# Diagonal score blocks as 64 by 64 squares, and the order of all steps written out as a list

## The chip, the cores and the metric

The kernel runs on one core of one Trainium2 chip. The metric is the device time of one execution in microseconds, the median over several runs.

## The reference

Two layers, each an attention A with a memory of earlier segments and then a feed-forward block B, on 2048 tokens of width 640:

```python
x = x + A(layernorm(x));  x = x + B(layernorm(x))      # and the same once more
# A: 32 heads of width 20, 4 segments of L = 512 tokens, M and z carried from segment to segment
logits = einsum('bhqd,bhkd->bhqk', qs, ks) * 20**-0.5 + mask    # causal within the segment
a_dot  = einsum('bhqk,bhkd->bhqd', softmax(logits), vs)
a_mem  = (phi(qs) @ M) / (phi(qs) @ z + 1e-6)          # phi(t) = t + 1 if t > 0 else exp(t)
o      = sigmoid(beta) * a_mem + (1 - sigmoid(beta)) * a_dot;   M += phi(ks).T @ vs;  z += sum phi(ks)
# B: relu(x @ w1) @ w2, hidden width 1728
```

## The kernel before

All activations are bf16 in SBUF; `x_sb` holds the tokens in 16 tiles of 128 partitions. Every step is a Python generator ("stream") that yields operations: scores, exponentials, causal masking, value sums, projections, memory reads and writes, the feed-forward block, loads and stores. A planner (`Sched`) holds a modelled clock per engine, picks at each step the stream whose operation can start first, moved by a hand-tuned table of shifts (`SHIFT`), and appends the operation to its engine's queue. What comes out is one fixed instruction order for TensorE (PE), VectorE (DVE), ScalarE (ACT), GpSimd (POOL) and SyncE (SP), with semaphores between them.

Matmuls come in three tile shapes of the 128 by 128 array. "Full" uses all of it. "cols" uses four column tiles of 32 (projections cut into quarters at L777, value sums at L1397): four matmuls side by side. "rows" uses four row tiles of 32 (scores at L1301): a head has 20 features, so four heads run side by side, each into its own PSUM bank. Projections and the feed-forward block exist as full (L774) and as four column tiles (L777), and the planner takes the shape that the array is in.

Scores are computed transposed: keys on partitions, queries on columns. A pair of groups (z = 0, 1; four heads each) takes five rounds; a round fills two slots of two PSUM banks with 512 columns per head:

```python
ROUNDS = (((0, 0, 0),), ((0, 1, 0), (0, 3, 384)), ((0, 2, 0), (1, 2, 256)),
          ((1, 0, 0),), ((1, 1, 0), (1, 3, 384)))        # (z, key block j, column in the bank)
```

Key block j of 128 keys is taken against the queries from 128*j on, so that a segment has 512 + 384 + 256 + 128 = 1280 columns per head. Per round ACT applies two exponentials (L1365, 128 partitions by 1024 elements) from PSUM into `PT`. POOL then zeroes the upper part of each diagonal 128 by 128 block (affine select, L1377), and the value sums (L1397) multiply `PT` by the values, four matmuls per key block, 16 per group. There are 32 pairs, 160 rounds. The two slots of a round have to be read by ACT before the next round can be written; a third slot is lent to the scores in the first segment only.

The scores read `pad`, to which SP copies q and k from a DRAM scratch `scr` (L1117), to which it copied the projections before (L1070). SP also issues the transposes, the weight loads (w1 at L643), the loads of x (L609, L618, L635) and the stores (L1642, L1646), all in the order of its own queue.

Of the kernel before, what the change touches and what calls it, by code (L numbers as in the profile page):

```python
# [7 lines left out]
ALU = mybir.AluOpType  # L8
# [27 lines left out]
PT_OFF = [0, 512, 1024, 896]  # L36
# [73 lines left out]
class Op:  # L110

    def __init__(self, alts, waits, dma=None, acq=None, urgent=False, take=(), mode="full", lag=0.0, port=False):
        self.lag = lag
# [8 lines left out]
        self.urgent = urgent  # L125
        self.take = take
        self.data = 0.0
# [32 lines left out]
class Spawn:  # L160
    def __init__(self, prio, gen):
        self.prio = prio
        self.gen = gen


LONE_NS = 300.0
SWITCH_NS = 96.0
COLS_LAG = 1500.0
SOFT = 400
SOFT_DMA = 1000  # L170
SOFT_FROM = ("sc",6,4,1)
SEM_NS = 60.0
PE_MARGIN = 80.0
HOLDERS = 1
SHIFT = {
# [41 lines left out]
}  # L217
HOLD_TOL = {"pe": 220.0, "act": 150.0, "dve": 200.0, "pool": 0.0, "sp": 0.0}


class Sched:


    def __init__(self, prog):
        self.P = prog
        self.free = {e: 800.0 for e in ENGS}
        self.t = {}
        self.events = {}
        self.streams = []
        self.dma_free = 0.0  # L230
        self.rank = {}
        self.mode = "full"
        self.soon = 0.0
        self.landed = set()
        self.met = {}
        self.seen = {}
        self.phase = {}
        self.made = {}
        self.held = {"dve": [], "pool": []}

    def add(self, prio, gen):
        self.streams.append([prio, gen, None, None, False])
        self.rank[id(gen)] = 0
# [8 lines left out]
    def enter(self, gen, phase):  # L252
        if self.phase.get(id(gen)) != phase:
            self.phase[id(gen)] = phase
            self.made[id(gen)] = 0

    def place(self, n, gen):
        k = self.made.get(id(gen), 0)
        return n, self.phase.get(id(gen), 0), sum(k >= x for x in (6, 20, 60))

# [6 lines left out]
    def _fill(self, st):  # L267
        while st[2] is None and not st[4]:
            try:
                y = next(st[1]) if st[3] is None else st[1].send(st[3][0])  # L270
            except StopIteration:
                st[4] = True
                return
            st[3] = None
            st[2] = y

    def _settle(self, st):

        while True:
            self._fill(st)  # L280
            if st[4]:
                return False
            y = st[2]
            if isinstance(y, (Op, Either)):
                return True
            if isinstance(y, Spawn):
                self.add(y.prio, y.gen)
                self.rank[id(y.gen)] = self.rank[id(st[1])]
                st[2], st[3] = None, (None,)
            elif isinstance(y, Need):  # L290
                if y.key not in self.events:
                    return False
                st[2], st[3] = None, (self.events[y.key],)
            else:
                s = self._pick(y.slots)
                if s is None:
                    return False
                s.free = False
                st[2], st[3] = None, (s,)
# [5 lines left out]
    def _mode(self, op):  # L305
        if op.cols is None:
            return op.mode
# [1437 lines left out]
```

## Time and profile before

| | |
|---|---|
| time, median of 3 runs | 551.09 us (550.83 to 551.12) |
| span of the profiled execution | 549.3 us |
| PE busy | 539.8 us, 98% |
| ACT busy | 406.0 us, 74% |
| DVE busy | 427.8 us, 78% |
| POOL busy | 195.7 us, 36% |
| score matmuls (L1301) | 1024 |
| exponentials (L1365) | 320, 1028 ns each |

The profiled execution has no time of its own besides its span, from the first to the last instruction; the runs' times also contain what lies around it. Busy PE time is the union of matmul records, which are pipelined: a record holds the columns and a tail, so that two neighbours overlap, and a busy PE may do less than it could. What a matmul occupies is read from the distance between starts. PE is idle mostly in the first 20 us.

### The profile page before, as it was taken

How to read it: one execution, taken by the hardware profiler on the slowest of the kernel's cores; microseconds unless marked ns; L12 is line 12 of the kernel's file. 1: busy time of each engine (PE TensorE's matmuls, PEld its weight loads, DVE VectorE, ACT ScalarE, POOL GpSimd, SP SyncE). 2: the span in 40 equal slices, each digit the busy share in tenths (PEclk: the TensorE clock that was granted, in tenths of full speed). 3: DMA queues.
4: the chain of work that ended last, by engine and by line, in shares of the span. 5: the costliest groups of instructions: out<-in, count | busy, mean ns of one | idle time of the engine just before them, and what ended most of it. 6: DMA issues, size and time to landing. Idle time of an engine off the chain costs nothing.

```text
span 549.3 us, 20483 instructions
## 1 busy us (share of the span) xinstructions
PE 539.8 (98%) x9025; PEld 305.5 (56%) x9025; DVE 427.8 (78%) x1067; ACT 406.0 (74%) x516; POOL 195.7 (36%) x305
## 2 busy tenths in 40 slices
PE   7999999999999999999999999999999999999997
PEld 6543464455554546646556555564646654757656
DVE  4899999898999989898778858997899788417102
ACT  5699899789888987788888867897778787350130
POOL 5255444333453334443433423433333333201000
PEclk9999999999999999999999999999999999999999
DMA  8699979715384175438384743336246511541201
GB/s 270 165 198 253 245 158 223 221 44 116 89 165 98 40 180 77 75 68 120 47 212 93 116 116 93 58 69 104 50 139 130 117 32 22 106 63 33 71 2 51
DMA packets 133325, 62.20 MB, mean 113 GB/s; under 512 B 112116, under 2 KB 123124, under 8 KB 133236
## 3 DMA queue, kind: packets, MB, share of 16 engines
q1 hardware_dynamic: 132672, 60.36, 51.5%
q8 instruction: 71, 1.16, 0.9%
q10 hardware_dynamic: 564, 0.53, 0.4%
q14 instruction: 18, 0.15, 0.1%
HBM read 20.56 MB, written 12.85 MB: 61 GB/s over the span
## 4 chain that ended last, share of the span: by engine, by line
PE 88%; ACT 6%; DVE 2%; DMA 2%; SPq 1%; issue 0%
PE ps L774 35%; PE ps L777 35%; PE ps L1301 8%; PE ps L1397 6%; ACT PT L1365 5%; PE ps L1180 2%; DMA x_sb<-in_A_x_dram 1%; PE ps L1572 1%; PE ps L1238 1%; DMA pad<-scr 1%; SPq L602 1%; DVE xn_tok L841 0%; SPq L612 0%; DVE stats L795 0%; DVE x_sb L1614 0%; DVE o_sb L1491 0%
## 5 line engine op out<-in xcount | busy, mean ns | idle before, releaser
L1365 ACT ACTIVATE PT<-ps 128x1024 bf16<-128x1024 f32 x320 | 308.9, 1028 | 59.3 <-PE ps L1301 57.6
L1377 POOL TENSOR_SCALAR_AFFINE_SELECT PT<-PT 128x512 bf16<-128x512 bf16 x256 | 169.3, 679 | 241.1 <-ACT PT L1365 241.0
L777 PE MATMUL ps<-xnT,w_r 128*32 128x512 bf16 x1256 | 76.0, 379 | 0.0
L777 PE MATMUL ps<-w_r,hT 128*32 128x320 bf16 (+1 forms) x1764 | 67.8, 295 | 0.0
L1614 DVE TENSOR_TENSOR x_sb<-x_sb,ps 128x320 bf16<-128x320 bf16 (+1 forms) x65 | 30.7, 474 | 43.6 <-PE ps L777 38.7
L1301 PE MATMUL ps<-pad 20*128 20x512 bf16 (+3 forms) x1024 | 63.4, 301 | 1.2 <-ACT PT L1365 0.7
L774 PE MATMUL ps<-w_r,hT 128*128 128x320 bf16 x404 | 64.2, 300 | 0.0
L795 DVE BATCH_NORM_STATS2 stats<-x_sb 128x6 f32<-128x320 bf16 x124 | 55.0, 478 | 3.8 <-DMA x_sb<-in_A_x_dram 3.0
L777 PEld LDWEIGHTS ps<-w_r,hT 128*32 128x32 bf16 x1764 | 45.2, 97 | 12.6 <-issue 1.4
L1595 ACT ACTIVATE hT<-ps 128x512 bf16<-128x512 f32 x50 | 29.9, 599 | 29.0 <-PE ps L777 25.6
L774 PE MATMUL ps<-xnT,w_r 128*128 128x512 bf16 x206 | 50.8, 380 | 0.0
L774 PEld LDWEIGHTS ps<-w_r,hT 128*128 128x128 bf16 x404 | 37.6, 98 | 19.4 <-issue 4.9
L1301 PEld LDWEIGHTS ps<-pad 20*128 20x128 bf16 x1024 | 17.9, 92 | 52.9 <-issue 24.5
L777 PEld LDWEIGHTS ps<-xnT,w_r 128*32 128x32 bf16 x1256 | 31.6, 97 | 27.8 <-issue 2.0
L1519 DVE TENSOR_TENSOR x_sb<-x_sb,ps 128x320 bf16<-128x320 bf16 x64 | 29.7, 478 | 20.4 <-PE ps L777 16.0
L811 POOL TENSOR_TENSOR rstd<-lnU,mhalf 128x2 f32<-128x2 f32 (+2 forms) x27 | 21.1, 782 | 63.5 <-DVE lnU L807 60.4
L1407 DVE CAST otu<-ps 128x512 bf16<-128x512 f32 x52 | 35.6, 685 | 9.1 <-PE ps L1397 8.2
L1397 PE MATMUL ps<-PT,v_aug 128*21 128x128 bf16 (+3 forms) x896 | 40.3, 300 | 0.0
L1594 DVE TENSOR_SCALAR hT<-ps 128x512 bf16<-128x512 f32 x54 | 36.5, 681 | 1.7 <-PE ps L774 0.7
L1491 DVE TENSOR_TENSOR o_sb<-otk,rden 128x320 bf16<-128x320 bf16 x62 | 34.8, 588 | 0.5
L981 DVE CAST stg<-ps 128x512 bf16<-128x512 f32 (+1 forms) x37 | 24.7, 669 | 12.5 <-PE ps L774 6.3
L1146 ACT ACTIVATE stg<-stg 128x512 bf16<-128x512 bf16 x50 | 31.7, 635 | 2.0 <-DVE rtmp L1144 1.8
(118 smaller groups left out, 731.5 us busy)
## 6 DMA issues: line engine op xcount, KB each, us to landing
pad<-scr SPq DMA_DIRECT2D x124, 80.0 KB
scr<-stg SPq DMA_DIRECT2D x34, 256.0 KB, 2.5
out_dram<-x_sb SPq DMA_DIRECT2D x15, 160.0 KB, 1.9
w_r<-in_B_w_dram SPq DMA_DIRECT2D x10, 216.0 KB, 4.0
w_r<-in_B_w_dram SPq DMA_DIRECT2D x13, 160.0 KB, 2.8
x_sb<-in_A_x_dram SPq DMA_DIRECT2D x10, 160.0 KB, 3.2
scr<-w_r SPq DMA_DIRECT2D x5, 256.0 KB, 4.2
wv_r<-in_A_wv_dram SPq DMA_DIRECT2D x1, 800.0 KB, 9.7
```

Of the source, the lines that this page charges most:

```text
L774: return e.matmul(view(dst.ap, b), a, b, start=(k == 0), stop=(k == last))
L777: return e.matmul(view(dst.ap[rows], b), part, b, start=(k == 0), stop=(k == last))
L795: tk = yield dve(320, 1, lambda e, c2=c2: e.bn_stats(stats6[:, t, c2, :], x_sb[:, t, c2 * 320:(c2 + 1) * 320]), xt)
L1146: te = yield act(512, lambda e, q=q: e.activation(q, q, ACT.Exp), [tr] + p, psum=False)
L1301: fns.append([(lambda e, z=z, j=j, hh=hh, N=N, o=o, sl=sl, q=hh % 2: e.matmul(slot.ap[:, q, o:o + N], sl.ap[32 * hh:32 * hh + DH, z, 0, 12 ...
L1365: tx = yield act(1024, lambda e, dst=dst, src=src: e.activation(dst, src, ACT.Exp, scale=SCALE), sc + pw)
L1377: tm = yield pool(600.0, lambda e, reg=reg: e.affine_select(out=reg, in_=reg, pattern=[[0, 4], [1, 128]], compare_op=ALU.is_ge, fill=0.0, ...
L1397: fns.append((lambda e, OD, j=j, hh=hh: e.matmul(OD.ap[32 * hh:32 * hh + DH + 1, 128 * j:L], VAUG[vx(a, s)][:, j, 4 * g + hh, :], pt.ap[:, ...
L1407: te = yield evac(L, 1, lambda e: e.tensor_copy(dst, OD.ap), lambda e: e.activation(dst, OD.ap, ACT.Copy), [tk] + OTU[0].tks)
L1491: to = yield dve(320, 1, lambda e, z=z, dst=dst: e.tensor_tensor(dst, av[:, z, :, :, 0:DH], rd.ap[:, z].to_broadcast([128, NJ, 4, DH]), AL ...
L1594: th = yield evac(512, 1, lambda e: e.tensor_scalar(hT[:, dc, :], bk.ap[:, :], 0.0, None, ALU.max), lambda e: e.activation(hT[:, dc, :], b ...
L1614: ta = yield dve(n, 1, lambda e: e.tensor_tensor(x_sb[:, t, c0:c0 + n], x_sb[:, t, c0:c0 + n], bk.ap[:, 0:n], ALU.add), [tk], urgent=True)
```

## The change

**Squares.** The diagonal block of 128 by 128 is cut into four squares of 64 by 64, and the one in which all keys are later than all queries is not computed any more. The rounds of a pair now are: two for z = 0, one shared round with the eight pairs of diagonal squares of both groups, two for z = 1. A square is a matmul of 64 keys by 64 queries in a 32 by 64 tile ("halves": four row tiles by two column tiles), 32 of them in the shared round. So that the squares of an even and an odd key block lie on different halves of the partitions, the odd token tiles are kept with their two halves swapped, from the load of x to the store of the result; each affected load or store is split by partition halves.

**Buffers.** `PT` keeps 1280 columns per head, in another order, and the squares that are not computed are cleared to zero once (two POOL memsets). The shared round's exponentials are four of 512 elements on 64 partitions, in place of two of 1024 on 128. POOL makes eight selects per pair as before, on blocks of 64 columns. The value sums take five segments of 512, 128, 256, 256 and 128 columns, 20 matmuls for 16.

**Order.** The planner's choice, its table of shifts and its priorities are gone. A string `ORDER` lists the number of the stream that goes next at each step, and whether it takes its second form (another engine, or column tiles). The model of the clock stays, for the choice among free buffers.

The built programs have 9025 and 11807 matmuls: the scores' go from 1024 to 2304, the value sums' from 992 to 1240, and 400 full matmuls of the projections and the feed-forward block become four column tiles each (1359 full at L774 before, 959 after).

```diff
-PT_OFF = [0, 512, 1024, 896]
+PT_AT = {(0, 0): 0, (0, 1): 128, (0, 2): 256, (0, 3): 384, (3, 3): 512, (2, 2): 640, (2, 3): 768,
+         (1, 2): 896, (1, 3): 1024, (1, 1): 1152}
+SUMS = ((0, 0, 512, 0), (3, 512, 128, 384), (2, 640, 256, 256), (1, 896, 256, 256), (1, 1152, 128, 128))
+FULLS = (((0, 64, 448), (3, 384, 64)), ((2, 320, 192), (1, 256, 256), (1, 128, 64)))
+FULL_AT = (64, 704)
+DIAG = ((0, 0, 0), (0, 3, 448), (1, 2, 256), (1, 1, 192))
...
+ORDER = """
+37*2 36*3 37 35 37 36 37*2 36 35 37 21*3 35 21 26 21*3 26 22*2 21 22 26*3 37*3 22 28*2 21 37 28*2 21 28 23*2 148 28*5
...
+        blocks = PT[:].rearrange("p z h (y c) -> p z (h y) c", y=2)
...
+        def pair_loads(t):
+            return [lambda e, p=p: e.dma_start(x_sb[p:p + 64, t:t + 2, :], bass.AP(
+                tensor=A_x.tensor, offset=A_x.offset + (128 * t + p) * D,
+                ap=[[D, 64], [(192 if p == 0 else 64) * D, 2], [1, D]])) for p in (0, 64)]
...
+            t2 = yield pool(1200, lambda e: e.memset(blocks[:, :, :, 0:64], 0.0))
+            t3 = yield pool(1200, lambda e: e.memset(blocks[:, :, :, 576:640], 0.0))
...
-        ROUNDS = (((0, 0, 0),), ((0, 1, 0), (0, 3, 384)), ((0, 2, 0), (1, 2, 256)),
-                  ((1, 0, 0),), ((1, 1, 0), (1, 3, 384)))
+        ROUNDS = ((0, 0), (0, 1), (None, None), (1, 0), (1, 1))
...
+                if zn is None:
+                    parts = [(z, 64 * (j % 2), q0, 64, q0, 64, 256 * y + 64 * z) for z in range(2) for y, j, q0 in DIAG]
+                else:
+                    parts = []
+                    for j, q0, nq in FULLS[w]:
+                        parts.append((zn, 0, 128 * j, 128, q0, nq, o))
+                        o += nq
...
-                    return pe(233.0, fns, a[1] + b[1] + a[0].tks + b[0].tks, take=[a[0], b[0]], mode="rows"), None
+                    on = ROUNDS[HALVES[h][1]][0] is None
+                    return pe(135.0 if on else 233.0, fns, a[1] + b[1] + a[0].tks + b[0].tks, take=[a[0], b[0]],
+                              mode="halves" if on else "rows")
...
+                        if z is None:
+                            src = bkp.ap.rearrange("p h (y x) -> p (h y) x", y=2)[:, :, 0:128].rearrange(
+                                "p e (z c) -> p z e c", z=2)
+                            moves = [(blocks[rows, :, 4 * k:4 * k + 4, c0:c0 + 64], src[rows])
+                                     for rows, c0 in ((slice(0, 64), 0), (slice(64, 128), 576))]
...
+            def clear(z, rows, c0, base, ex):
+                reg = blocks[rows, z, :, c0:c0 + 64]
+                return pool(600.0, lambda e: e.affine_select(
+                    out=reg, in_=reg, pattern=[[0, 2 * 4], [1, 64]], compare_op=ALU.is_ge, fill=0.0, base=base,
+                    channel_multiplier=-1), ex)
...
-            for j in range(NJ):
+            for y, (j, c0, nq, q0) in enumerate(SUMS):
                 for hh in range(4):
...
-            OD, tk = yield pe(540.0, fns, mk + vt, acq=MISC, mode="cols", lag=COLS_LAG)
+            OD, tk = yield pe(545.0, fns, mk + vt, acq=MISC, mode="cols")
```

More of the change, by code (lines that the diff above doesn't have):

```diff
@@ L110, with __init__ @@
 class Op:
-    def __init__(self, alts, waits, dma=None, acq=None, urgent=False, take=(), mode="full", lag=0.0, port=False):
-        self.lag = lag
+    def __init__(self, alts, waits, dma=None, acq=None, take=(), mode="full", port=False):
         self.port = port
@@ L454, in pe, with _times @@
-def pe(ns, fns, waits=(), acq=None, take=(), mode="full", lag=0.0):
-    return Op([("pe", ns, fns, 190.0)], waits, acq=acq, take=take, mode=mode, lag=lag)
+    def _times(self, op, k, waits):
+        e, hold, fns, tail = op.alts[k]
+        m = PE_MARGIN if e == "pe" else 0.0
+        if e == "pe" and op.mode == "cols" and op.cols_ns is not None:
+            hold = op.cols_ns
+        if e == "pe" and op.mode != self.mode:
+            hold = hold + SWITCH_NS
+        start = max([self.at(t) + SEM_NS + m for t in waits], default=0.0)
+        start = max(self.free[e], start)
+        if e == "dve" and op.port:
+            for a, b in self.held["pool"][-6:]:
+                if a <= start + 66.0 < b:
+                    hold = max(hold, b - start + op.data - 70.0)
+        if e == "pool":
+            for a, b in self.held["dve"][-6:]:
+                if a < start + hold and b > start:
+                    hold = hold + b - max(a, start)
+        return start, start + hold
@@ new lines, in run @@
+    def run(self):
+        tops = list(self.streams)
+        first = tops[0]
+        self._settle_all()
+        for word in ORDER.split():
+            code, _, count = word.partition("*")
+            for _ in range(int(count or 1)):
+                n, other = int(code) % 80, int(code) >= 80
+                st = tops[n] if n < 40 else next(x for x in self.kids[id(tops[n - 40])] if not x[3])
+                self._record(st, st[1].fn() if isinstance(st[1], Either) else st[1], other)
+                self._settle(st)
+                self._settle_all()
+                if isinstance(first[1], Either):
+                    first[1].fn()
+        assert not self.streams
@@ new lines, in _record @@
+    def _record(self, st, op, other):
+        k = int(other and len(op.alts) > 1)
+        e, _, fns, tail = op.alts[k]
+        if op.cols is not None:
+            op.mode = "cols" if other else "full"
+            fns = op.cols if other else fns
+        waits, slot = op.waits, None
+        for s in op.take:
+            s.free = False
+        if op.acq is not None:
+            slot = self._pick(op.acq)
+            slot.free = False
+            waits = waits + slot.tks
+            fns = [(lambda eng, fn=fn, slot=slot: fn(eng, slot), mark) for fn, mark in fns]
+        start, end = self._times(op, k, waits)
+        self.P.waits(e, waits)
+        self.free[e] = end
+        if e == "pe":
+            self.mode = op.mode
+        if e == "dve" and op.port:
+            self.held[e].append((end - op.data, end))
+        elif e == "pool":
+            self.held[e].append((start, end))
+        if op.dma is not None:
+            tk = self.P.dma(e, fns[0][0], op.dma)
+            self.dma_free = max(self.dma_free, start + 300.0) + tail[1]
+            self.t[(id(tk[0]), tk[1])] = max(self.dma_free, end) + tail[0]
+            if tail[2]:
+                self.free[e] = max(end, self.dma_free)
+            out = tk
+        else:
+            marks = []
+            for fn, mark in fns:
+                tk = self.P.op(e, fn, mark)
+                if tk is not None:
+                    self.t[(id(tk[0]), tk[1])] = end + tail
+                    marks.append(tk)
+            out = marks[0] if len(marks) == 1 else (marks or None)
+        st[1], st[2] = None, ((slot, out) if slot is not None else out,)
@@ L458, in either, with pe @@
+def pe(ns, fns, waits=(), acq=None, take=(), mode="full"):
+    return Op([("pe", ns, fns, 190.0)], waits, acq=acq, take=take, mode=mode)
 def either(op, cols, ns=None):
@@ L617, in loads @@
                     yield Need("warmed")
-                yield from ld(("sp", "act")[t // 2], "x0%d%d" % divmod(t, 2), 163840, lambda e, t=t: e.dma_start(
-                    x_sb[:, t, :], xs[:, t, :]))
+                tks = []
+                for fn in one_load(t):
+                    tk = yield dma(("sp", "act")[t // 2], sem_("d_x0%d%d" % (t, len(tks))), 81920 if t % 2 else 163840,
+                                   fn, lat=1470.0)
+                    tks.append(tk)
+                S.set("x0%d%d" % divmod(t, 2), tks=tks)
             tz = yield Need("beta0")
@@ L633, in x_pieces @@
             def x_pieces(s):
-                def one(t):
-                    return lambda e: e.dma_start(x_sb[:, t, :], xs[:, t, :])
-                return [("x%d%d" % (s, i), 163840, one(4 * s + i)) for i in range(4)]
+                return [("x%d%d" % (s, i), 163840, fn) for i in range(2) for fn in pair_loads(4 * s + 2 * i)]
             def rows(name, w, src, k):
@@ L933, in proj_ln @@
             if a == 0:
-                xw = [[("x10",)]] * 2 + [[("x11",)]] * 2 if s == 1 else [[("x%d%d" % (s, i),)] for i in range(NJ)]
+                xw = [[("x10",)]] * 2 + [[("x11",)]] * 2 if s == 1 else [[("x%d%d" % (s, i // 2),)] for i in range(NJ)]
             else:
@@ L1286, in half @@
                 m, u, k = HALVES[h]
-                parts = ROUNDS[u]
+                zn, w = ROUNDS[u]
                 pd = []
-                for z in {z for z, _, _ in parts}:
+                for z in range(2) if zn is None else (zn,):
                     n = 2 * m + z
@@ L1352, in exps @@
                         pts.append(pt)
-                    pw = [t for z, _, _ in parts for t in pts[z].tks]
+                    pw = [t for pt in (pts if z is None else pts[z:z + 1]) for t in pt.tks]
                     ex = []
@@ L1609, in ffn @@
             hrest = yield Need("hR", b, s)
-            sums = [[] for _ in range(NJ)]
             def residual(i, hf, bk, tk, c0, n):
@@ new lines, in store @@
+            if s < NSEG - 1:
+                return
+            t = TT - 2
+            tks = yield Need("xB", b, s, NJ - 2)
+            S.last = yield dma("sp", dout, 163840, lambda e, t=t: e.dma_start(
+                out[0, t * 128:(t + 1) * 128, :], x_sb[:, t, :]), tks)
+            t, i = TT - 1, NJ - 1
+            for hf, u, c0, n in ((0, 0, 0, 320), (1, 0, 320, 160), (2, 0, 480, 160)):
+                tks = yield Need("sum", b, s, 2 * i + hf)
+                for k, (p, r) in enumerate(halves(t)):
+                    S.last = yield dma(("sp", "act")[k], dout, 128 * n, lambda e, p=p, r=r, c0=c0, n=n: e.dma_start(
+                        out[0, t * 128 + r:t * 128 + r + 64, c0:c0 + n], x_sb[p:p + 64, t, c0:c0 + n]), tks)
@@ new lines, in items @@
+        def items(f, count):
+            for n in range(count):
+                yield from f(n)
+        S.add(scores())
+        S.add(exps())
+        S.add(items(causal, NSEG * G))
+        S.add(items(apply, 2 * NSEG * G))
+        S.add(each(free_v))
+        S.add(items(turn_pair, NSEG * G))
+        S.add(items(divide, NSEG * G))
+        S.add(each(turn_o))
+        S.add(each(out_proj(0)))
+        S.add(each(out_proj(1)))
+        S.add(each(ln_b(0)))
+        S.add(each(ln_b(1)))
+        S.add(each(fill))
@@ L1712, in bass_interleave_layers__memory_aug_infini_attn__dense_activation_relu__prompt_kernel @@
+        S.add(each(proj_v))
+        S.add(each(ffn))
+        S.add(each(ffn_rest))
+        S.add(each(store))
+        S.add(warm_pe())
+        S.add(consts())
+        S.add(loads())
+        S.add(late_loads())
         S.run()
```

594 lines of the change are left out of this document (262 added, 332 removed), and 41 rows, old and new, of the table SHIFT.

## The prediction, made before the changed kernel ran

> **What bounds the kernel now.** I read the page's parts 1, 2 and 4 first, then the windows view, then the timeline of TensorE alone.
>
> ```profile
> span 549.3 us, 20483 instructions
> PE 539.8 (98%) x9025; PEld 305.5 (56%) x9025; DVE 427.8 (78%) x1067; ACT 406.0 (74%) x516; POOL 195.7 (36%) x305
> PEclk9999999999999999999999999999999999999999
> PE 88%; ACT 6%; DVE 2%; DMA 2%; SPq 1%; issue 0%
> ```
>
> TensorE (PE) is busy 98% at the full clock, and the chain that ended last is 88% PE. The three runs have a median of 551.09 us, 1.8 above this span; I make the sum against the span and carry the 1.8 over.
>
> ```profile
> 0.00:20.00 20.00, 16.37 (x162) 12.50 (x162) 12.06 (x36) 9.89 (x27) 8.06 (x26) 1.00 0.73 223
> 20.00:31.00 11.00, 11.00 (x126) 5.77 (x122) 10.48 (x31) 10.36 (x15) 4.97 (x7) 1.00 0.95 204
> 31.00:65.00 34.00, 32.19 (x462) 14.31 (x457) 31.70 (x79) 32.10 (x37) 19.16 (x29) 1.00 1.02 240
> 65.00:75.00 10.00, 9.76 (x81) 5.46 (x82) 9.80 (x25) 8.85 (x12) 3.35 (x5) 1.00 0.98 189
> 75.00:150.00 75.00, 75.00 (x1098) 40.19 (x1096) 68.53 (x170) 65.47 (x82) 30.84 (x47) 1.00 0.60 139
> 150.00:470.00 320.00, 319.19 (x5111) 175.08 (x5114) 273.24 (x678) 260.47 (x316) 126.63 (x188) 1.00 0.49 98
> 470.00:546.00 76.00, 76.00 (x1996) 52.13 (x2000) 21.65 (x54) 18.82 (x31) 2.69 (x5) 1.00 0.23 49
> ```
>
> The first number after each stretch's length is PE's busy time. Outside the first 20 us PE is idle 1.81 us in 31 to 65, 0.24 in 65 to 75, 0.81 in 150 to 470, and nowhere else. So the kernel is PE's own work plus three microseconds. Only 31 to 65 has another limit: ScalarE (ACT) is busy 32.10 of 34 there, and the chain of waits is ACT for nearly all of it:
>
> ```profile
> 33.96 25.71 ACT PT L1365 x28
> 59.67 0.10 SPq L643
> ...
> 59.81 0.43 SPq L1070
> 60.28 0.43 SPq L1070
> ...
> 60.76 4.43 DMA pad<-scr
> ...
> 65.24 0.39 PE ps L1301 x4
> ```
>
> 28 exponentials back to back, then a `pad` transfer that is issued only behind a piece of w1 and two `scr` stores on SP, and lands at 65.19. A busy PE may still waste array time, so its cost per step is read from starts:
>
> ```profile
> 300.66 0.59 PE L774 MATMUL ps<-xnT,w_r 128*128 128x512 bf16 x2
> 301.19 0.39 PE L1301 MATMUL ps<-pad 20*128 20x512 bf16 x4
> 301.51 0.73 PE L1572 MATMUL ps<-xnT,w_r 128*32 128x256 bf16 x20
> 304.34 2.33 PE L774 MATMUL ps<-xnT,w_r 128*128 128x512 bf16 x10
> ...
> L774 PE MATMUL ps<-xnT,w_r 128*128 128x512 bf16 x206 | 50.8, 380 | 0.0
> ```
>
> Ten 512-column matmuls take 2.33 us, the last one 0.38 (the mean in the last row: 0.21 of columns and a tail of 0.17): 0.217 between starts, which is 2.4 columns per ns (213 ns) and 3 ns. Two of them from 300.66 are done feeding at 301.09; the score matmuls start at 301.19, and four of them side by side (32-row tiles) let the next tile shape start 0.32 later, not 0.22. **A change of tile shape costs about 0.10 us each way**: 0.10 in, 0.107 out.
>
> **The change, part by part.** Counts are from the order of the two built programs; 32 pairs of head groups, five score rounds each, four heads side by side.
>
> *Squares.* Round 2 had 512 columns in two waves of four matmuls (256 and 256); now 32 matmuls of 64 columns, eight side by side if the 32 by 64 tiles run together: four waves, 256 columns, 107 ns of array time less. But a wave costs more than its columns:
>
> ```profile
> 181.30 0.29 PE L1301 MATMUL ps<-pad 20*128 20x256 bf16 x4
> 181.42 0.28 PE L1301 MATMUL ps<-pad 20*128 20x256 bf16 x4
> 147.31 0.33 PE L1238 MATMUL ps<-v_aug,phk 128*32 128x42 bf16 x24
> ```
>
> A wave of 256 columns in row tiles (107 ns) is followed 0.12 later by the next: 13 ns over. In column tiles (third row: six waves of four, 42 and 63 columns, each matmul with its own weights) 24 matmuls take 0.33; less the last one's 0.19 (a tail of 0.17 and its columns) that is 0.14 for five steps, 28 ns each where the columns need 26. So weights reload at that pace, and the excess lies between 2 and 13 ns a wave. The squares have both kinds of tile, and a round that is over at a wave's last matmul; I take the row tiles' 13, the nearest, for each of three inner steps and 13 more for the eight matmuls' stagger. New round: 107 + 39 + 13 = 159 ns; old: 213 + 13 = 226. Gain 67 ns, times 32: **-2.15 us**. At 3 ns a step without stagger it is 116 ns (-3.5); if the two 64-column halves do not run together, eight steps of 27 + 13 make 320 ns (+3.0).
>
> *The other rounds* keep 512 columns in more waves: 448 and 64 for one of 512, 192, 256 and 64 for 384 and 128. One step of 13 ns more in each of 4 x 32 rounds: **+1.66** (bounds 0.26 at 2 ns, 3.4 at twice 13).
>
> *Shape changes*: 322 before, 330 now, the eight more between full and column tiles: 8 x 0.10, **+0.8** (bounds 0 and 0.9).
>
> *Value sums* (L1397): five segments of the same 1280 columns for four, 62 times, 3 ns: **+0.2**. Full matmuls turned into four column tiles keep their columns: nothing.
>
> *ScalarE.* The square round's two exponentials of 1024 become four of 512 on 64 partitions.
>
> ```profile
> L1365 ACT ACTIVATE PT<-ps 128x1024 bf16<-128x1024 f32 x320 | 308.9, 1028 | 59.3 <-PE ps L1301 57.6
> 329.05 1.94 ACT L1365 ACTIVATE PT<-ps 128x1024 bf16<-128x1024 f32 x2 [0.81 <-PE ps L1301]
> L982 ACT ACTIVATE stg<-ps 128x512 bf16<-128x512 f32 x30 | 18.0, 600 | 5.4 <-PE ps L777 3.1 <-PE ps L774 1.8
> 331.39 0.40 PE L1301 MATMUL ps<-pad 20*128 20x512 bf16 x4
> 331.72 1.53 PE L774 MATMUL ps<-wv_r,xnT 128*128 128x320 bf16 x10
> 331.82 1.94 ACT L1365 ACTIVATE PT<-ps 128x1024 bf16<-128x1024 f32 x2 [0.51 <-PE ps L1301]
> 334.22 0.40 PE L1301 MATMUL ps<-pad 20*128 20x384 bf16 x8
> ```
>
> Two take 1.94, so the next starts after 0.91 and 0.12 of each is hidden; 512 at 600 ns then steps by 0.48. Four: 1.92, two: 1.82, **0.1 us more per pair, 3.3 us of ACT in all, hidden**: the score matmuls end earlier by 0.07, and the rows show the cover: the exponentials of 331.82 end at 333.76 and the next round starts at 334.22, 0.46 later. With that cover gone PE would pay up to 3.3. Where ACT does set the pace (31 to 65, 14 rounds, three of them squares) it is 0.3, and the new order has two ACT copies fewer ahead of round 16, at 0.48 each: nil.
>
> *GpSimd.* Eight selects of 512 elements per pair as before (two on 64 partitions), and two clearings of 1024 elements once. For group 0 two selects now follow the square round's exponentials, where one did: 0.68 later for its value sum.
>
> ```profile
> L1377 POOL TENSOR_SCALAR_AFFINE_SELECT PT<-PT 128x512 bf16<-128x512 bf16 x256 | 169.3, 679 | 241.1 <-ACT PT L1365 241.0
> 9.51 0.73 POOL L701 MEMSET maskg<- 128x756 bf16 x1 [0.68 <-DVE xn_tok L853]
> 20.29 1.94 ACT L1365 ACTIVATE PT<-ps 128x1024 bf16<-128x1024 f32 x2
> 0.80 0.87 SPq L618 DMA_DIRECT2D x_sb<-in_A_x_dram  x2
> 3.00:4.00 1.00, 1.00 (x13) 1.00 (x11) 0.89 (x2) 0.00 (x0) 0.00 (x0) 1.00 1.02 341
> ```
>
> POOL waits 241 us for ACT in all, and the list puts full or column matmuls ahead of the value sum; 0. The clearings, estimated at 1 us each from the 756 elements in 0.73, stand ahead of the mask work at 9.51; the first exponentials, which now wait for them, come at 20.29: 0.
>
> *Transfers.* Odd token tiles come and go half-swapped, so the second tile's load is two DMAs: one issue more on SP (0.87 / 2 = 0.43) ahead of the first weights, which PE waits for. But the DMA engines are full from 3 us on (share 1.02), so landing goes by bytes, which are the same: **+0.1** (0 to 0.43). Stores: the same bytes; SP issues 18 stores for 17 and ACT three for one, and the last piece is halved over two queues: 0.
>
> *The order.* The scheduler's choice is replaced by a list. By PE work counted ahead of each score round, the two programs agree within 0.8 us nearly everywhere, so most of it is the old order. Two places differ. Between rounds 8 and 19 (38 to 59 us) the new list puts up to 1.6 us more PE work ahead of the ACT-paced rounds, where PE pauses. And on SP the first `pad` transfers of the second segment stand ahead of the `scr` stores that preceded the last of them, and ahead of six of the ten w1 pieces that all went first, so the landing at 65.19 should come earlier. The pauses show as 1.81 us of idle, and each hides up to 0.17 more under the previous matmul's tail. I take **-1.9** of it (bounds 0 and -2.9). Of the 1.05 us later, **-0.3** (bounds -1 and +1).
>
> Sum: -2.15 + 1.66 + 0.8 + 0.2 + 0.1 - 1.9 - 0.3 = **-1.6**: span 547.7, time **549.5**.
>
> By the Trainium skill ("TensorE: Matmul & The Clock Gate", Part 3) a pack of tiles spans one matmul and about 4 ns for each further tile. For four row tiles the trace agrees (13 ns); for eight squares it gives a rival, next.
>
> **Rivals.** *Each wave waits for all eight tiles.* Starts of a wave are 3.3 ns apart in row tiles (13 over four); if the next wave waits for the eighth, a step is 27 + 26 = 53 ns and the round 213 + 13 = 226: no gain at all. Sum +0.55, time 551.6. For it: row tiles behave so; against it: column tiles do not. Chance 0.12.
>
> *The halves exclude each other* (slower): 320 ns a round, 161 more than I take, times 32 = +5.2: 554.7. It is slower than now by 0.2% from 243 ns a round on. For it: no row of before has tiles split both ways; against it: row tiles and column tiles each run four at a time. Chance 0.13.
>
> *The list gives nothing*: the pauses of 31 to 65 stay, since ACT sets them: 551.4. For it: the positions agree so well. Against: the SP order did change at the transfer that ended the chain. Chance 0.16.
>
> *ACT's cover is gone*: strided 64-partition exponentials cost more than 0.48 and the square rounds hold PE: up to +3.3, 552.8. Chance 0.05.
>
> **How the numbers follow.** My forecast has 0.54. Two programs of this kernel can be told apart from about 0.2% on, 1.1 us: faster is below 549.99, slower above 552.19. The forecast's own range, with squares between 116 and 175 ns and the list between -2.9 and -1, is 547.2 to 550.8, nine tenths of it faster. Faster: 0.49 from it, 0.06 from the list giving nothing with cheap squares, 0.02 from the first rival with the pauses gone: 0.57. Slower: 0.13 + 0.05 and 0.03 of the others: 0.21. Same: 0.22. The range 546.8 to 553.0 leaves out the halves' exclusion and a little below.
>
> **What would show it.** The squares' wave: starts of the 64-column matmuls four or eight apart by 30 to 53 ns, and PE's next tile shape 0.25 to 0.30 us after the first of them. In 31 to 65 PE's idle under 0.8 us, and the first score round of the second segment before 64. ACT about 3 us busier, with its waits for scores shorter by as much. I am wrong if the squares' round is over 0.24 us, or if PE's idle past 75 us grows beyond 2.

## The result, and the profile after

The changed kernel takes 567.04 us (median, 565.65 to 569.46) against 550.96 for the kernel before in the same runs: 1.0299 times as long, 95% interval 1.0273 to 1.0325. I had predicted 549.5, in a range to 553.0. The profiled execution is the longest one, 569.46 us with a span of 567.7. Further below, one of the third experiment's four executions took 896.19 us at a mean granted clock of 0.557 and is left out of the ratio and interval given there (561.39 is the median with it, 561.26 without).

The page of the changed kernel, parts 1, 2 and 4:

```profile
span 567.7 us, 26129 instructions
PE 545.9 (96%) x11807; PEld 324.3 (57%) x11807; DVE 422.6 (74%) x1067; ACT 418.2 (74%) x580; POOL 199.1 (35%) x307
PEclk8999999999999999999999999998999999999999
PE 67%; DVE 12%; ACT 12%; DMA 6%; issue 1%; SPq 1%; POOL 0%; DVEq 0%
```

The chain of waits is only 67% PE (88% before). PE is idle for 21.8 us (567.7 less 545.9) where it was 9.5, and it is busy 6.1 us longer (539.8 before). ACT is 12 us busier (406.0 before), where I had 3.3. The same stretches as before, in the windows view:

```profile
0.00:20.00 20.00, 15.95 (x149) 13.13 (x150) 11.88 (x31) 8.89 (x23) 7.01 (x20) 0.91 0.77 200
20.00:31.00 11.00, 10.53 (x153) 5.38 (x154) 10.09 (x28) 9.02 (x15) 5.62 (x12) 1.00 0.95 177
31.00:65.00 34.00, 31.20 (x661) 14.39 (x659) 31.05 (x76) 32.83 (x43) 19.09 (x28) 1.00 0.85 203
65.00:75.00 10.00, 9.69 (x239) 5.61 (x235) 8.93 (x24) 9.48 (x15) 4.67 (x7) 1.00 0.85 132
75.00:150.00 75.00, 70.71 (x1344) 39.87 (x1345) 61.89 (x149) 62.99 (x86) 28.59 (x43) 1.00 0.72 154
150.00:470.00 320.00, 313.18 (x6961) 182.74 (x6960) 250.06 (x646) 269.41 (x367) 122.45 (x182) 0.99 0.49 98
```

Idle PE time is now everywhere: 4.3 us in 75 to 150, where there was none, and 6.8 in 150 to 470, where there was 0.8. No one place lost the time. The granted clock (the third number from the end) is 0.91 in the first 20 us and 0.99 in 150 to 470: it stood at half for 3.4 us in each, which makes PE's busy time longer by up to 1.7 us each. What the squares themselves do is in the timeline of PE and of ACT around one pair:

```profile
177.01 0.33 PE L1321 MATMUL ps<-pad 20*64 20x64 bf16 x32
177.28 0.39 PE L788 MATMUL ps<-xnT,w_r 128*128 128x512 bf16 x1
...
180.00 0.40 PE L1321 MATMUL ps<-pad 20*128 20x448 bf16 x8 [0.23 <-ACT PT L1387]
...
177.50 2.44 ACT L1387 ACTIVATE PT<-ps 64x512 bf16<-64x512 f32 x4 [0.23 <-PE ps L1321]
179.97 0.60 ACT L994 ACTIVATE stg<-ps 128x512 bf16<-128x512 f32 x1
```

The squares' round is over in 0.27 us, up to the start of the next tile shape. The kernel before needed 0.33 for the two waves of 256:

```profile
181.30 0.40 PE L1301 MATMUL ps<-pad 20*128 20x256 bf16 x8
181.63 0.39 PE L774 MATMUL ps<-xnT,w_r 128*128 128x512 bf16 x1
```

But its four exponentials last from 177.50 to 179.94, 2.44 us; a round's two had lasted 1.94. The next score round needs the banks, and waits 0.23 us behind full matmuls that the list had put there as cover. The same in sum, from the waits view (us in total, times, longest), first after:

```profile
PE ps L1321 <- ACT PT L1387: 5.7, 21, 0.8
PE ps L880 <- DVE xn_tok L867: 2.6, 2, 2.2
PE ps L791 <- DMA xnT<-xn_tok: 1.8, 1, 1.8
```

and then before, the row that answers to the first:

```profile
PE ps L1301 <- ACT PT L1365: 0.7, 2, 0.5
```

Score rounds now wait for exponentials 21 times and not twice.

### The profile page after: what moved, and what is told of

It reads as the page before. It is cut to its first block, busy times and chain, and to the rows that moved or that the text cites. A ratio compares the mean times of both kernels' runs of the same rounds, so it can differ in the third digit from the quotient of the medians.

```text
span 567.7 us, 26129 instructions
## 1 busy us (share of the span) xinstructions
PE 545.9 (96%) x11807; PEld 324.3 (57%) x11807; DVE 422.6 (74%) x1067; ACT 418.2 (74%) x580; POOL 199.1 (35%) x307
## 4 chain that ended last, share of the span: by engine, by line
PE 67%; DVE 12%; ACT 12%; DMA 6%; issue 1%; SPq 1%; POOL 0%; DVEq 0%
PE ps L791 37%; PE ps L788 16%; ACT PT L1387 10%; PE ps L1321 7%; PE ps L1432 5%; DVE xn_tok L855 2%; DMA xnT<-xn_tok 2%; DMA x_sb<-in_A_x_dram 1%; PE ps L1191 1%; DVE stats L809 1%; ACT stg L1157 1%; DVE phs L1158 1%; DVE o_sb L1526 1%; DMA otk<-otu 1%; DVE otu L1442 1%
## 5 line engine op out<-in xcount | busy, mean ns | idle before, releaser
L1387 ACT ACTIVATE PT<-ps 128x1024 bf16<-128x1024 f32 (+1 forms) x384 | 323.7, 882 | 56.9 <-PE ps L1321 52.8
L1396 POOL TENSOR_SCALAR_AFFINE_SELECT PT<-PT 128x512 bf16<-128x512 bf16 (+1 forms) x256 | 171.0, 696 | 257.4 <-ACT PT L1387 257.4
L791 PE MATMUL ps<-w_r,hT 128*32 128x320 bf16 (+1 forms) x2424 | 101.8, 297 | 0.0
L791 PE MATMUL ps<-xnT,w_r 128*32 128x512 bf16 x1484 | 94.3, 385 | 2.2 <-DMA xnT<-xn_tok 1.8
L1321 PE MATMUL ps<-pad 20*64 20x64 bf16 (+4 forms) x2304 | 61.6, 226 | 6.2 <-ACT PT L1387 5.7
L1321 PEld LDWEIGHTS ps<-pad 20*128 20x128 bf16 (+1 forms) x2304 | 27.6, 98 | 55.8 <-ACT PT L1387 32.3
L788 PE MATMUL ps<-w_r,hT 128*128 128x320 bf16 x239 | 42.1, 299 | 0.0
L1432 PE MATMUL ps<-PT,v_aug 128*21 128x128 bf16 (+2 forms) x1120 | 40.5, 273 | 0.2 <-issue 0.2
L791 PE MATMUL ps<-wo_r,oT 128*32 128x320 bf16 x700 | 36.9, 300 | 0.0
L1432 PEld LDWEIGHTS ps<-PT,v_aug 128*21 128x21 bf16 x1120 | 25.4, 93 | 14.2 <-issue 1.2
```

Of the source, the lines that this page charges most:

```text
L788: return e.matmul(view(dst.ap, b), a, b, start=(k == 0), stop=(k == last))
L791: return e.matmul(view(dst.ap[rows], b), part, b, start=(k == 0), stop=(k == last))
L1321: fns.append([(lambda e, z=z, p=p, k0=k0, nk=nk, q0=q0, nq=nq, o=o, hh=hh, sl=sl, q=hh % 2: e.matmul(slot.ap[p:p + nk, q, o:o + nq], sl.ap ...
L1387: tx = yield act(1024 // len(moves), lambda e, dst=dst, src=src: e.activation(dst, src, ACT.Exp, scale=SCALE), sc + pw)
L1396: return pool(600.0, lambda e: e.affine_select(out=reg, in_=reg, pattern=[[0, 2 * 4], [1, 64]], compare_op=ALU.is_ge, fill=0.0, base=base, ...
L1432: fns.append((lambda e, OD, y=y, j=j, c0=c0, nq=nq, q0=q0, hh=hh: e.matmul(OD.ap[32 * hh:32 * hh + DH + 1, q0:q0 + nq], VAUG[vx(a, s)][:, ...
```

## Experiments

In all of them the kernel before ran beside; its median was 550.5 to 550.9.

### Is it the list or the squares?

The order in which the kernel before records its steps can be written down as a list and given to the changed kernel, and the other way round. Where a pair of exponentials or a load is four or two instructions in the one and fewer in the other, the entry is doubled or dropped.

```diff
 # first: the changed kernel
-ORDER = <its list>
+ORDER = <the order that the planner of before records>
 # second: the kernel before
-SHIFT = {...}; <the planner's choice>
+ORDER = <the list of the changed kernel>; value sums of group 0 may go after its own four selects
```

> The squares, with their exponentials, selects and swapped tiles, but the steps in the order in which the kernel before records them (its own choice of engine and tile shape at each step, too). Theory L (the list leaves no slack: it makes TensorE wait wherever an engine is later than planned): the +16 us go, 549 to 552 us. Theory P (the pace of ScalarE: the four exponentials on 64 partitions start 616 ns apart where I took 480, so a square round holds ScalarE 2.46 us for 1.82, 20 us over 32 pairs): the loss stays, 560 to 568, and score rounds after squares wait for ScalarE as in the changed kernel.

> The kernel before with its old rounds, exponentials and loads, but its steps in the order of the changed kernel's list (two of the four exponentials of a square round and the doubled loads dropped from the list). Theory L: 562 to 567 us. Theory P: the list is harmless by itself, 549 to 553.

Squares in the old order: 570.26 us, 1.0355 (1.0313 to 1.0396). Old rounds in the new order: 554.08, 1.006 (1.0035 to 1.0086). Theory L falls. The list costs 3.2 us by itself (1.9 to 4.7 by the interval); the larger part is there with the squares under either order: 19.3 us above the kernel before in the old one, 13.0 above the old rounds in the new one.

The page of the old rounds in the new order (an execution of 552.92 us) shows where the list's share lies:

```profile
span 550.9 us, 22995 instructions
PE 542.3 (98%) x10279; PEld 309.6 (56%) x10279; DVE 418.8 (76%) x1067; ACT 402.5 (73%) x516; POOL 193.0 (35%) x305
```

PE is idle for 8.6 us there, no longer than before (9.5), but busy for 2.5 longer. Eight more changes of tile shape are 0.8 of that. The matmuls that became four column tiles each are not the rest: four column tiles of 512 columns follow four others after 216 ns (median), as one full matmul follows another. A wait shorter than a matmul's tail counts as busy time; whether such waits are the rest isn't shown.

The waits view of the squares in the old order:

```profile
PE ps L1354 <- ACT PT L1420: 10.6, 38, 0.6
PE ps L1465 <- POOL PT L1429: 3.5, 6, 1.4
```

38 score rounds wait for exponentials. The second row, value sums that wait for the selects, is not in the changed kernel, whose list puts these sums later.

### What makes the four exponentials slow?

In the changed kernel's trace the four start 616, 618 and 616 ns apart (medians of 32 rounds), each is 593 long, and whatever follows the fourth starts 617 after it. So none overlaps with its neighbour, while two of 1024 on 128 partitions start 0.92 apart (median) at 1.03 each. Two edits:

```diff
 # third experiment
-moves = [(blocks[rows, :, 4*k:4*k+4, c0:c0+64], src[rows]) for rows, c0 in ((0:64, 0), (64:128, 576))]
+moves = [(blocks[:, :, 4*k:4*k+4, c0:c0+64], src) for c0 in (0, 576)]
 # fourth experiment
-for k in range(2): for rows in (upper, lower): exp(slot k, rows)
+for rows in (upper, lower): for k in range(2): exp(slot k, rows)
```

> The changed kernel, its list untouched; the four exponentials of a square round run on all 128 partitions, 512 elements each, instead of 64 (the other half of the partitions gets scores that belong elsewhere, so the diagonal blocks' sums are not the reference's). Theory P with the partitions as its cause: steps of 0.48 us, a square round's exponentials over in 2.0 us, and the time comes down by about 10 to 14 us, to 552 to 557. If the strides or the list are the cause: steps stay at 0.6 and the time at 565 to 567. Theory L: the steps change, the time stays above 562.

> The changed kernel with the four exponentials of a square round in another order: both slots' upper halves, then both lower halves, so that the partition half changes once and not three times. If the change of the half is what keeps two exponentials from overlapping: two of three steps at 0.48 us, some 8 us less in all, 558 to 562. If 64 partitions by themselves are slow: steps of 0.616 throughout and 565 to 567.

On 128 partitions: steps of 494, 478 and 478, 561.39 us, 1.0149 (1.0091 to 1.0206). Upper, upper, lower, lower: steps of 494, 603 and 498, and 603 to the instruction behind, 561.74 us, 1.0203 (1.0162 to 1.0244). The timeline of ACT at the same round, in the third experiment

```profile
339.72 2.06 ACT L1386 ACTIVATE PT<-ps 128x512 bf16<-128x512 f32 x4
```

and in the fourth:

```profile
338.61 2.17 ACT L1386 ACTIVATE PT<-ps 64x512 bf16<-64x512 f32 x4
```

So 64 partitions and strides are not slow in themselves (494 and 498 within one half). It is the change of partitions between two neighbours, upper to lower, lower to upper or lower to all, that takes the overlap away: about 0.12 us each time. The changed kernel has four such changes in a round. The step from all 128 partitions to the upper half, with which each square round begins, is not one of them: behind an exponential of 1086 ns the first of the four starts after 904, behind an instruction of 598 ns after 494. So in all these pairs the overlap is there when both instructions begin at the same partition (0 or 64), and not when they don't. The time came down by 5.7 and 5.3 us, less than the 10 to 14 and 8 that I expected, so ScalarE's pace isn't the whole loss. The 5.7 is uncertain: the two ratios make it 8.3 (1.0299 less 1.0149, of 551 us), and the one execution of each kernel at a mean clock of 1.0 makes it 8.0 (565.65 less 557.66).

### Each suspect put into the kernel before, and the pace taken out another way

```diff
 # fifth: kernel before, its order replayed      # sixth: the same, tiles 1 and 3
-exp(128 partitions x 1024)                      -dma_start(x_sb[:, t, :], xs[:, t, :])
+exp(0:64, 512); exp(64:128, 512)                +for p in (0, 64): dma_start(x_sb[p:p+64, t, :], xs[p:p+64, t, :])
 # seventh and eighth: squares in the old order, in the new order
-for k in range(2): for rows in (upper, lower): exp(slot k, rows)
+for rows in (upper, lower): exp(both slots, rows)        # 64 x 1024, two in all
```

> The kernel before in its own order, with one edit: in every pair but the first, the two exponentials of round 2 (1024 elements on 128 partitions) become four of 512 on 64 partitions, upper and lower half in turn, as in the changed kernel; half of the shared round's scores stay unread. No squares, no swapped tiles. Theory P (ScalarE's pace alone): the step is 0.616 us, the round behind it waits for ScalarE 0.3 to 0.4 us in most pairs as with the squares in the old order (10.6 us of such waits in the first experiment), so 561 to 566 us. If the squares' other parts carry the loss (selects, halved loads, more matmuls): under 556.

> The kernel before in its own order, with the loads of token tiles 1 and 3 each cut into two transfers of 64 partitions, as in the changed kernel but not swapped. Theory S (the start): the statistics of tile 1 start about 2 us later (6.6 for 4.4 us in the changed kernel), VectorE holds everything behind them, and the time is 552 to 553.5 us. If only the bytes count, as I predicted: 551.0 to 551.4.

> The first experiment (squares in the old order) with the square round's four exponentials merged into two, one for each half of the partitions, 1024 elements over both slots: two steps of about 0.95 and 1.03 us for four of 0.616, so that the round's exponentials take about 2.0 us as before the change; both slots come free at the end of the second. Theory P: 554 to 558 us, of which 2 are the start and the rest the later selects and the slots' later release. If ScalarE's pace is not the cause: 566 to 570.

> The changed kernel in its own order with the same two merged exponentials. Theory P: as cheap as with all 128 partitions (561) or a little below, 556 to 561; what stays above 551 is the list's own 3 us (second experiment) and the start's 2. If the two slots' later release costs as much as the pace gives back: 563 to 567.

The four exponentials in the kernel before: 557.58 us, 1.0118 (1.0096 to 1.0139), so +6.9: less than theory P alone asked (561 to 566), more than the other theory's under 556, and much more than the 0.1 us a pair that I had counted and hidden. The halved loads of tiles 1 and 3: 552.47, 1.0029 (1.0015 to 1.0043), +1.8. Merged exponentials: 562.91 in the old order, 1.0209 (1.0185 to 1.0233), 7.4 less than the first experiment; 563.7 in the new, 1.0233 (1.0198 to 1.0268), 3.3 less than the changed kernel. I had asked 554 to 558 and 556 to 561. The merged pair steps at 1.04 us, again without overlap, the round's exponentials take 2.06, and both slots come free only at its end; in the new order that is the case that I had put at 563 to 567.

How a halved load costs 2 us is in the timeline of VectorE. Before, the statistics of tile 1 were

```profile
4.44 0.89 DVE L795 BATCH_NORM_STATS2 stats<-x_sb 128x6 f32<-128x320 bf16 x2 [0.22 <-DMA x_sb<-in_A_x_dram]
```

and in the sixth experiment:

```profile
4.08 0.21 DVE L896 BATCH_NORM_AGGREGATE mv<-stats 128x2 f32<-128x12 f32 x1
5.86 0.89 DVE L894 BATCH_NORM_STATS2 stats<-x_sb 128x6 f32<-128x320 bf16 x2 [1.57 <-DMA x_sb<-in_A_x_dram]
6.78 0.21 DVE L896 BATCH_NORM_AGGREGATE mv<-stats 128x2 f32<-128x12 f32 x1
6.91 0.39 DVE L952 TENSOR_SCALAR xn_tok<-x_sb,mv,rstd 128x640 bf16<-128x640 bf16 x1
```

VectorE waits 1.57 us for the second half of tile 1, and the normalization of tile 0 (L952), for which PE waits, stands behind that wait in its queue. So tile 1 in two halves is complete 1.4 us later than whole (5.86 for 4.44). The transfers are half as large and land later. From the view of the DMA issues (KB each, median us to landing), ACT's queue, before (tiles 2 and 3, 2.8 and 3.7 us)

```profile
x_sb<-in_A_x_dram ACTq DMA_DIRECT2D x2, 160.0 KB, 3.2
```

and after (the halves of tile 3):

```profile
x_sb<-in_A_x_dram ACTq DMA_DIRECT2D x2, 80.0 KB, 4.6
```

The Trainium skill ("DMA: Bandwidth & Descriptors", Rules for kernel authors) advises against two transfers to disjoint partition halves, since both run over the same engines one after the other, and for one of 128 partitions. The trace bears the advice out: tile 3 takes 4.6 us for 3.7, tile 1 is complete 1.4 later.

The wait need not be all of the 1.8 us. Behind it TensorE's clock goes to half, in the sixth experiment

```profile
7.36 0.45 PE L965 MATMUL ps<-om_sb,xn_tok 128*128 128x128 bf16 x5 [1.99 <-DVE xn_tok L952]
9.58 0.74 PE L873 MATMUL ps<-xnT,wq_r 128*128 128x128 bf16 x5
```

```profile
9.00:10.00 1.00, 1.00 (x12) 1.00 (x10) 0.67 (x2) 0.00 (x0) 0.73 (x2) 0.50 1.08 344
```

and before:

```profile
5.94 0.45 PE L866 MATMUL ps<-om_sb,xn_tok 128*128 128x128 bf16 x5 [0.62 <-DVE xn_tok L853]
9.56 0.44 PE L774 MATMUL ps<-xnT,wq_r 128*128 128x128 bf16 x5
```

Five matmuls take 0.74 us for 0.44. The granted clock (0.50 in the windows view's row) is at half from 8.3 to 11.7, and all seven executions of the sixth experiment have a mean clock of 0.997, nine of ten of the kernel before beside them 1.0. The traces of all fourteen kernels agree: with halved loads PE's last matmuls at half pace in the start come at 10 to 14 us, with whole ones at 4 to 7. How much of the 1.8 us is the wait and how much the clock the runs don't separate.

### Both side costs away

```diff
 # ninth: changed kernel, whole tiles loaded, not swapped (tiles 1 and 3, the pairs, the late pieces)
-pair_loads: two transfers of 64 partitions by 2 tiles
+one transfer of 128 partitions by 2 tiles (late pieces: by one tile)
 # tenth: the same, and the exponentials of the third experiment
```

> The changed kernel with the loads of before (whole tiles, not swapped: the causal mask then falls wrongly in the odd tiles, which changes no time). Theory S: the start gains back its 1.8 us (sixth experiment) and the four paired loads, which hold SP 0.73 us each in halves, some 1 to 2 us more: 563 to 565.5 us. If halved loads cost at the start alone and only there: 565 to 566.

> The same with the square round's exponentials on all 128 partitions as in the third experiment: no slow ScalarE, no halved loads; what is left of the change is the squares on TensorE, the value sums in five segments, the selects and the list. If pace, loads and list add up: 557 to 559.5 us (561.4 less 2 to 4). If the list's 3 us is the whole rest and the squares give their 2 us: 552 to 555. If something else in the squares costs (selects on GpSimd, more matmuls): above 560.

Old loads: 563.09 us, 1.0223 (1.0208 to 1.0237). With the exponentials on 128 partitions as well: 555.48, 1.0085 (1.0072 to 1.0098), between two of my ranges. So, taken out in this order, the loads cost 4.0 us (567.04 less 563.09), twice what they cost the kernel before, and ScalarE's pace 7.6. The 4.0 contains the clock too: the ninth's four executions all have a mean clock of 1.0, the changed kernel's 0.994 to 1.0. Most of it lies at the start: the first score round comes at 21.33 us in the changed kernel's trace and at 18.29 in the ninth's. What is left of the change stays 4.7 us above the kernel before. In this tenth kernel PE waits at a few fixed places:

```profile
PE ps L832 <- DMA xnT<-xn_tok: 2.0, 2, 1.7
PE ps L832 <- DVE v_aug L1088: 1.4, 2, 1.0
PE ps L829 <- DVE phs L1199: 1.2, 1, 1.2
PE ps L787 <- DVE beta_z L793: 1.2, 1, 1.2
PE ps L1362 <- ACT PT L1427: 1.1, 2, 0.8
```

The fourth row is PE's first wait, 1.1 to 1.2 us in every kernel; the others are steps that the list puts where their transfers, copies and exponentials aren't yet done. The list alone doesn't make these waits: with the old rounds in the same order those for `xnT` and `v_aug` are 0.7 and 0.4 us in all. Against the kernel before PE is idle for 4.2 us longer (13.7 for 9.5) and busy for 0.8 longer (540.6 for 539.8).

### The selects

> The squares in the order of before, with both side costs taken away: exponentials on all 128 partitions and whole, unswapped loads (the masks of odd tiles fall wrongly). What is left of the change is TensorE's squares, the value sums' fifth segment and the selects. If pace and loads are all that the squares cost: the first experiment's 570.3 less 7 and 4, and less again what I predicted the squares to give, 549 to 552 us. If the selects cost too (two of 0.69 us behind the square round for group 0 where one was; 3.5 us of value sums waiting for GpSimd in the first experiment): 554 to 558.

> The same, with group 0's second select of the square round cut from 512 elements to 64 (that part of the mask is left out). If GpSimd's selects delay the value sums: their waits for GpSimd go, and the time comes down by 2 to 4 us from the run beside it. If not: within 1 us of it.

```diff
 # twelfth: of the two selects for group 0 behind the square round, the second
-affine_select(64 columns of all 8 blocks)
+affine_select(64 columns of 1 block)
```

Squares alone in the old order: 559.26 us, 1.0162 (1.0142 to 1.0182), above both of my ranges. With the short select 554.82, 1.0098 (1.006 to 1.0135): 4.4 us less. The value sums' waits for GpSimd, in the eleventh

```profile
PE ps L1463 <- POOL PT L1427: 3.3, 5, 1.2
```

and in the twelfth:

```profile
PE ps L1464 <- POOL PT L1428: 0.8, 1, 0.8
```

In the order of before the second select does cost, 4.4 us, of which these waits show 2.5. In the changed kernel no such wait is among its listed ones, since its list has the sums later. 4.3 us stay here too, as 4.7 do in the new order. No version that I ran is faster than the kernel before, not even these two with parts left out.

## Why the prediction was wrong

**The squares were right.** From a score round's first start to the next tile shape, medians of 32: 326, 328, 330, 326, 328 ns before, 327, 330, 262, 327, 330 after. The square round gives 68 ns, 2.2 us in all (-2.15 predicted). The rivals that hung on its pace, 226 and 320 ns, fall: the 0.27 us lies within the 0.25 to 0.30 that I gave. The other rounds lose 1 to 2 ns each, 0.2 us in all, not the 13 ns and 1.66 us. The closeness of 2.2 to 2.15 is partly luck: the four waves start 52, 32 and 32 ns apart (medians) where I had 40 three times, so the first of them does behave as the rival had it (53 ns).

**The step that failed first is ScalarE: "0.1 us more per pair, 3.3 us of ACT in all, hidden".** I took the step of 512-element copies on 128 partitions, 0.48, for exponentials that alternate between two halves. It is 0.616, so that a square round occupies ACT for 2.46 us where two of 1024 take 1.82: 20 us in all instead of 3.3. The cover of 0.46 us I had found, and named what it would cost once gone; the round's exponentials now last 0.50 longer, and the cover is a little too short in most pairs. Taken out, the pace is worth 7.6 us in the new order (5.7 to 8.3 with the halved loads still there); put into the kernel before, it costs 6.9. My rival "ACT's cover is gone" had the mechanism, with a price of at most 3.3 and a chance of 0.05. What no row of before could show is two neighbours that begin at different partitions, and I gave no bound for it from above: with no overlap at all, four of 600 ns, the rows that I quoted would have given 2.4.

**The second is "Transfers +0.1 (0 to 0.43)"**, measured as 4.0. "Landing goes by bytes" failed: tile 1 in two halves is complete 1.4 us later than whole. And I counted SP's issue time, but not who stands behind a late tile in VectorE's queue, nor that TensorE's clock falls behind the wait. In the order of before that was 1.8 us; in the changed kernel's trace 3.0 us are lost before the first score round. What the paired and late loads add isn't shown.

**The third is "The order -1.9 ... -0.3"**, which measures +3.2 with the old rounds. PE's idle time in 31 to 65 is 2.80 us, not under 0.8, and the first score round of the second segment starts at 67.54, not before 64. With the old rounds in the new order these are 0.83 us (1.81 before) and 62.54: so the list does shorten those pauses, by 1.0 of the 1.9, and the SP queue did move the round. What it costs lies elsewhere, in 2.5 us more of PE's busy time, where I had only the 0.8 of the shape changes. Counting PE work ahead of each round showed that two orders are alike for PE; it doesn't show how late each step's inputs are.

**Right or nearly:** shape changes (0.10 to 0.12 us each way, 330 of them), GpSimd at 0 for this list, though not for the old one, where the selects cost 4.4. My sign to look for, "PE's idle past 75 us grows beyond 2", is what came.

**The sum:** 4.0 for the loads, 7.6 for the pace and 4.7 for the rest make 16.3 (567.04 less the 550.76 beside the tenth experiment), by construction, since each was taken out of the one before. Of the 4.7, about 3 would be the list, if it costs as much with the squares as with the old rounds; that isn't shown, and in the old order, without the list, 4.3 us stay as well. Why the squares' own 2 us on PE don't appear in the time is open: in the tenth kernel they are not in PE's busy time either (540.6 us for 539.8), and what takes them back the runs don't show.

## What to carry to other kernels

A change that saves time on the engine that bounds the kernel has to be costed on every engine that reads its output: here 2 us on PE were bought with 20 on ACT, which had 0.46 us to spare in each pair. When a change cuts one instruction or one transfer in two by partitions, the price of the pieces can't be read from whole ones. Bound the instructions by the sum of their full durations, and ask who stands behind the pieces in the same queue. An order that is tuned to a kernel holds little slack, so it has to be made anew, or at least looked at, once a step's duration moves by half a microsecond.

## What the runs showed of the hardware

**ScalarE overlapped two neighbours only when both began at the same partition.** Starts are 478 to 498 ns apart (medians) from 128 to 128 partitions or within one half and 494 from all 128 to the upper half, 603 to 618 from the upper half to the lower, back, or from the lower half to all, for instructions of 578 to 616 ns. The pair of the upper half and then all doesn't occur. The Trainium skill ("ScalarE: Activation LUTs", What ACT_TABLE_LOAD costs) has an overlap of 93 ns between neighbours, without this condition; these traces show about 0.12 us and, across a change of the first partition, none.

**TensorE's clock fell to half behind a wait of 1.8 us, but not behind each such wait.** In the changed kernel's windows view, around its longest wait past the start (a transpose that lands at 384.0):

```profile
382.00:383.00 1.00, 0.25 (x12) 0.05 (x4) 1.00 (x4) 0.71 (x1) 0.00 (x0) 1.00 0.66 19
383.00:384.00 1.00, 0.00 (x0) 0.00 (x0) 0.93 (x4) 1.00 (x2) 0.00 (x0) 1.00 0.40 83
384.00:385.00 1.00, 0.97 (x16) 0.44 (x20) 0.35 (x2) 0.23 (x1) 0.53 (x1) 0.89 1.18 246
385.00:386.00 1.00, 1.00 (x16) 0.45 (x12) 0.00 (x0) 0.27 (x1) 1.00 (x2) 0.50 0.85 277
386.00:387.00 1.00, 1.00 (x16) 0.40 (x12) 0.00 (x0) 0.85 (x2) 0.71 (x2) 0.50 0.04 14
387.00:388.00 1.00, 1.00 (x12) 0.17 (x4) 0.14 (x1) 0.00 (x0) 0.00 (x0) 0.50 0.00 0
388.00:389.00 1.00, 1.00 (x48) 0.56 (x48) 1.00 (x3) 0.33 (x1) 0.00 (x0) 0.91 0.00 0
```

The column behind the engines' busy times is the granted clock. It falls to half at about 384.8 for 3.4 us, while PE works again, so that the wait costs up to 1.7 us more after it is over. The other such stretch is from 9.3 to 12.7, behind a wait of 2.2 us. The fastest of the changed kernel's executions, 565.65, has a mean clock of 1.0, the profiled one, with two stretches at half, 0.994. In the eighth experiment a wait for the same transposes lasts 1.77 us and the pace stays: behind it eleven steps of four column tiles take 2.56 us, 0.217 each and a tail.

```profile
380.57 2.56 PE L831 MATMUL ps<-xnT,w_r 128*32 128x512 bf16 x44 [1.77 <-DMA xnT<-xn_tok]
```

The Trainium skill ("TensorE: Matmul & The Clock Gate", Part 1) gives windows of about 3.4 us, which agrees with the dip's length, and a fall after one or more idle windows. Here PE worked for nearly half of the 3.4 us before the fall, and idled for 1.8.
